# Fused attention and two gated layers on one core: partial outputs kept apart until the last layer, gated values split out of PSUM, and new costs in the planner

## The chip, the core and the metric

The kernel runs on one core of a Trainium2 chip. The metric is device time in microseconds (us) of one execution. The core has TensorE (PE, with PEld for its weight loads), VectorE (DVE), ScalarE (ACT), GpSimd (POOL), and SyncE (SP), whose queue here issues nearly every DMA. Engines run their own instructions strictly in program order and wait for each other through semaphores.

## The reference

Three parts follow each other on float32 data; the weights arrive as float64.

```
q_rot, k_rot = rotate(q), rotate(k)                       # 4 batches, 8 heads, 576 tokens, 64 wide
attn = softmax(q_rot @ k_rot.T / 8);  x = attn @ v        # x: 2304 tokens x 512
gate = 1 / (1 + exp(-(x @ w_gate)));  val = x @ w_val     # 512 -> 1536
y = (gate * val) @ w_out                                  # 1536 -> 512
h = y @ w_in;  e = exp(h - max(h));  solu = h * e / sum(e)     # 512 -> 1024
ln = (solu - mean) / sqrt(var + 1e-6) * g_ln
out = ln @ w_out2                                         # 1024 -> 512
```

## The kernel before, in words

Every matmul operand is held as a high part and a low part, and each product is three matmuls (high by high, high by low, low by high). So each value that PE is to read costs two instructions: a cast that writes the high part, and a subtraction that writes the low part.

**Stage A** (0 to some 303 us) is attention and is not touched. Its output goes to memory as `xd`, in three blocks of 768 tokens.

**Stage B** (some 303 to 800 us) is the gated layer. The 1536 inner columns are done in three passes `s` of 512, each pass over three blocks `b`: nine blocks. A block has four units: the gate product of half of the columns, the value product of that half, and again both for the other half (`unit`). After the first block a unit is seven block products of a Strassen scheme (`product`, 42 matmuls of 384 columns), whose intermediate sums ACT copies out of PSUM (`hold`, line 994, tiles `held`) and DVE adds back in PSUM (`finish`, line 999, and line 1049). PSUM has two sets of four banks a to d: `near` for gate units, `far` for value units. ACT takes the sigmoid into `sg`; DVE multiplies the value bank into `sg` (line 1013), and `sg` is split into `gs`: the high part by ACT or DVE (line 487), the low part by POOL or DVE (line 1018). Then two outputs of 48 matmuls each (`output`) project the two halves of the block's tokens, the first in the near banks, the second in the far ones. For `s` = 0 ACT copies each output bank into one of six slots of `yst` (line 1085), which SP stores to memory as `yd` (line 1086). For `s` > 0 SP first loads the sum so far from `yd` into the slot (line 1082), DVE adds the bank (line 1083), and SP stores it again.

Between blocks SP loads the next block's `x` into `xst` (line 962), DVE forms Strassen differences (line 536), and the pieces are split into `xs` (541, 543 high, 545 low). At each new `s` the weights are decoded from float64 (464 on ACT; 467, 470, 475 on DVE), added (484) and split (487 high, 495 and 958 low).

**Stage C** (some 790 us to the end) is the last layer on 18 tiles of 128 tokens: load of `y` (1120), split (1129 high, 1131 low), 24 matmuls into `ph` ("H"), six steps of exponential and normalisation ("n", lines 1268 to 1292), a DMA transposition of packed halves ("P", "u"), and 24 matmuls into `po` ("J").

**Order.** In stage B and the start of C every instruction is a `job` with an engine, a cost, the spans it reads and writes and a due time; `run_jobs` replays the jobs with these costs and writes the program in that order. `AV` is a job that may go to ACT or DVE, `GV` one for POOL or DVE; it goes to whichever is free first by these costs. Stage C is then written by a string, `START`, and a loop over tiles.

Of the kernel before, what the change touches and what calls it, by code (L numbers as in the profile page):

```python
# [20 lines left out]
def kernel(  # L21
# [21 lines left out]
    nc = tc.nc  # L43
# [300 lines left out]
    def scale_x(i):  # L344
# [8 lines left out]
    xd, yd = (  # L353
        [hbm.tile([KD * P * BT], F32, name=f"{n}{b}").rearrange("(k p t) -> k p t", k=KD, p=P) for b in range(NB)] for n in ("xd", "yd")
# [492 lines left out]

    jobs, seen = [], {}

    def job(eng, took, fn, reads=(), writes=(), need=0.0):  # L850
# [8 lines left out]
        jobs.append((eng, took, fn, after, need))  # L859
# [33 lines left out]
    HURRY = 3.0  # L893
    raws_used = [0]

    def decode(kind, n, dst, dst_at, need):
# [14 lines left out]
    def make_sums(need):  # L911
        for n, (out, x, y, _) in enumerate(SUMS):
            job(V, 0.45, lambda n=n: w_sum(n, V), (w32_at(x), w32_at(y)), (w32_at(out),), need - 4)

    def make_splits(k, parts, need, of=None):
        for to, c in parts:
            at_ = to if of is None else of + to
            src, hi, lo = one("w32", at_, at_ + c), words_at(W_SLOTS[k], c, to), words_at(W_SLOTS[k], c, 1792 + to)
            job(AV, (0.1 + c / 1000, 0.08 + c / 1500), lambda e, to=to, c=c, at_=at_: w_high(slots[k], to, c, at_, e), (src,), (hi,), need - 3)
            job(GV, (0.2 + c / 430, 0.08 + c / 930), lambda e, to=to, c=c, at_=at_: w_low(slots[k], to, c, e, at_), (src, hi), (lo,), need - 2)  # L920
# [27 lines left out]
    def make_unit(kind, n, where, need):  # L948
# [8 lines left out]
        job(AV, (0.58, 0.42), lambda e: high(e, t[:, 0], val), (at_,), (hi,), need - 3)  # L957
        job(GV, (1.35, 0.62), lambda e: e.tensor_sub(out=t[:, 1], in0=val, in1=t[:, 0].bitcast(F32)), (at_, hi), (lo,), need - 2)

    def load_x(b, need):  # L960
        for kk in range(KD):
            job(SP, 1.3, lambda kk=kk: nc.sync.dma_start(out=xst[kk], in_=xd[b][kk]), (one(f"xd{b}"),), (one("xst", 2 * kk, 2 * kk + 2),), need - 6)
# [3 lines left out]
    def quarter_at(name, j):  # L966
        k, t = {"B11": (0, 0), "B12": (0, 1), "B21": (1, 0), "B22": (1, 1)}[name]
        return one("xst", 2 * (2 * k + j) + t, 2 * (2 * k + j) + t + 1)

    def split_x(need):  # L970
        for n, (name, at_, of) in enumerate(X_STEPS):
            for j in range(2):
                here = quarter_at(at_, j)
                if of is not None:
                    use = {2: 2, 4: 3, 6: 3, 8: 4}[n]
                    job(V, 0.5, lambda n=n, j=j: x_step(xst, n, j, t_eng=V), tuple(quarter_at(q, j) for q in of), (here,), need + use - 4)
# [200 lines left out]
    for c in range(12, 16):  # L1177
        make_unit("p", c % 8, C_AT[c], END + 40)
# [312 lines left out]
```

## Time and profile before

| | |
|---|---|
| time, three runs | 990.88, 992.06 (median), 995.15 us |
| the profiled execution, its own time | 995.61 us |
| span from its first to its last instruction | 993.8 us |
| busy: PE, PEld, DVE, ACT, POOL | 917.2, 854.8, 782.5, 620.2, 511.4 us |
| mean granted TensorE clock | 0.975 |

The profiled execution is 3.55 us above the median of the runs; 1.8 us of it lie around the span. A share of busy time is a mean over three stages with different limits, so the stages are read one by one.

### The profile page before, as it was taken

How to read it: one execution, taken by the hardware profiler on the slowest of the kernel's cores; microseconds unless marked ns; L12 is line 12 of the kernel's file. 1: busy time of each engine (PE TensorE's matmuls, PEld its weight loads, DVE VectorE, ACT ScalarE, POOL GpSimd, SP SyncE). 2: the span in 40 equal slices, each digit the busy share in tenths (PEclk: the TensorE clock that was granted, in tenths of full speed). 3: DMA queues.
4: the chain of work that ended last, by engine and by line, in shares of the span. 5: the costliest groups of instructions: out<-in, count | busy, mean ns of one | idle time of the engine just before them, and what ended most of it. 6: DMA issues, size and time to landing. Idle time of an engine off the chain costs nothing.

```text
span 993.8 us, 16167 instructions
## 1 busy us (share of the span) xinstructions
PE 917.2 (92%) x5368; PEld 854.8 (86%) x5368; DVE 782.5 (79%) x1298; ACT 620.2 (62%) x1288; POOL 511.4 (51%) x411
## 2 busy tenths in 40 slices
PE   5999999999999689997998988898999889999998
PEld 4999999989989679996998988797999868888886
DVE  6999999999885968599784879894779776666661
ACT  5999999889873535554743445461537656656662
POOL 7688898889562645475550547471437411112110
PEclk9999999999999889999999999999999899999999
DMA  5668777877626551424533251816054444544532
GB/s 138 154 174 214 189 196 190 219 187 180 179 81 210 172 165 53 137 76 144 180 100 112 73 160 47 274 63 202 12 166 141 155 106 97 122 89 98 115 69 48
DMA packets 128403, 136.33 MB, mean 137 GB/s; under 512 B 54832, under 2 KB 106304, under 8 KB 128320
## 3 DMA queue, kind: packets, MB, share of 16 engines
q1 hardware_dynamic: 128320, 135.30, 48.9%
q8 instruction: 42, 0.69, 0.3%
q14 instruction: 41, 0.34, 0.1%
HBM read 75.67 MB, written 25.76 MB: 102 GB/s over the span
## 4 chain that ended last, share of the span: by engine, by line
PE 57%; DVE 21%; DMA 8%; issue 7%; ACT 6%; POOL 0%; SPq 0%; DVEq 0%; ACTq 0%; POOLq 0%
PE s L292 8%; PE av L420 7%; PE te L379 5%; DVE xst L536 4%; PE po L1353 3%; PE po L1351 3%; PE po L1352 3%; DMA yd<-yst 2%; PE ph L1258 2%; PE ph L1256 2%; PE ph L1257 2%; DVE xs L545 2%; DVE w L484 2%; PE tq L219 2%; DVE sg L1013 2%
## 5 line engine op out<-in xcount | busy, mean ns | idle before, releaser
L1018 POOL TENSOR_TENSOR gs<-sg,gs 128x384 fp32r<-128x384 f32 x60 | 71.3, 1193 | 87.7 <-ACT gs L487 77.2
L304 ACT ACTIVATE e<-s,nm 128x576 f32<-128x576 f32 x144 | 107.5, 747 | 13.6 <-DVE nm L299 13.3
L299 DVE TENSOR_REDUCE nm<-s 128x1 f32<-128x576 f32 x144 | 107.2, 745 | 4.5 <-PE s L292 2.9
L373 DVE TENSOR_TENSOR et<-te,et 128x512 fp32r<-128x512 f32 x144 | 98.5, 685 | 12.6 <-ACT et L370 12.3
L292 PE MATMUL s<-st 128*128 128x288 f32 x512 | 100.0, 318 | 6.8 <-ACT e L304 5.3
L420 PE MATMUL av<-et,vs 128*128 128x288 f32 x512 | 100.0, 316 | 0.6 <-DVE uw L660 0.3
L545 POOL TENSOR_TENSOR xs<-xst,xs 128x384 fp32r<-128x384 f32 x71 | 84.5, 1208 | 31.1 <-ACT xs L541 14.0
L370 ACT CAST et<-te 128x512 fp32r<-128x512 f32 x144 | 84.1, 585 | 4.4 <-PE te L379 3.2
L379 PE MATMUL te<-ident,e 128*128 128x128 f32 x576 | 86.7, 274 | 0.0
L292 PEld LDWEIGHTS s<-st 128*128 128x128 f32 x512 | 74.4, 193 | 14.0 <-ACT e L304 9.9
L420 PEld LDWEIGHTS av<-et,vs 128*128 128x128 f32 x512 | 72.9, 189 | 4.3 <-DVE uw L660 2.8
L379 PEld LDWEIGHTS te<-ident,e 128*128 128x128 f32 x576 | 71.3, 142 | 0.1
L541 ACT CAST xs<-xst 128x384 fp32r<-128x384 f32 x97 | 47.0, 513 | 36.7 <-DVE xst L536 36.7
L1289 POOL TENSOR_TENSOR st<-st,mhalf 128x1 f32<-128x1 f32 x18 | 10.4, 579 | 100.2 <-DVE st L1288 100.2
L464 ACT ACTIVATE mag<-raw_w 128x512 f32<-128x512 f32 x52 | 34.7, 675 | 41.8 <-DMA raw_w<-in_moe_w_val_dram 18.7
L536 DVE TENSOR_TENSOR xst<-xst 128x384 f32<-128x384 f32 x64 | 59.4, 959 | 0.0
L495 POOL TENSOR_TENSOR wg<-w,wg 128x512 fp32r<-128x512 f32 (+2 forms) x16 | 24.6, 1539 | 56.5 <-ACT wg L487 37.0
L721 PE MATMUL near_a<-xs,wg 128*128 128x384 f32 x96 | 35.0, 364 | 16.7 <-ACT held L994 14.2
L487 ACT CAST gs<-sg 128x384 fp32r<-128x384 f32 x65 | 33.2, 515 | 25.7 <-DVE sg L1013 25.4
L1131 POOL TENSOR_TENSOR xs<-xst,xs 128x512 fp32r<-128x512 f32 x18 | 24.6, 1367 | 44.0 <-ACT xs L1129 43.4
L432 POOL TENSOR_TENSOR x_sb<-uw,um 64x576 f32<-64x576 f32 x30 | 43.7, 1456 | 3.3 <-DMA um<-uw 2.0
L169 POOL TENSOR_TENSOR turned_t<-raw_t,other_t 128x576 f32<-128x576 f32 (+1 forms) x30 | 43.7, 1479 | 1.2
(340 smaller groups left out, 3111.8 us busy)
## 6 DMA issues: line engine op xcount, KB each, us to landing
yd<-yst SPq DMA_DIRECT2D x72, 192.0 KB
st<-st SPq DMA_DIRECT2D x45, 288.0 KB
xst<-xd SPq DMA_DIRECT2D x32, 384.0 KB
raw_w<-in_moe_w_out_dram SPq DMA_DIRECT2D x20, 512.0 KB
yst<-yd SPq DMA_DIRECT2D x48, 192.0 KB
st<-st SPq DMA_DIRECT2D x47, 144.0 KB
raw_w<-in_moe_w_gate_dram SPq DMA_DIRECT2D x12, 512.0 KB
raw_w<-in_moe_w_val_dram SPq DMA_DIRECT2D x12, 512.0 KB
```

The lines of the kernel that those rows point to most:

```text
L169: op(out=turned[i][:, sl, hs, here].rearrange("p i h d -> p h i d"), in0=raws[i][:, hs, sl, here], in1=others[i][:, hs, sl, there],)
L292: nc.tensor.matmul(ps[:, j, :HALF], w, x, start=m == 0, stop=m == len(mm) - 1)
L299: nc.vector.tensor_reduce(out=nm, in_=ps[:, :, :HALF], axis=AX.XY, op=ALU.max, negate=True)
L304: nc.scalar.activation(out=e.rearrange("p (j c) -> p j c", j=2), in_=ps[:, :, :HALF], func=AF.Exp, bias=nm, accum_out=sums[i][:, n:n + 1],)
L370: nc.scalar.copy(out=h_out, in_=ps)
L373: nc.vector.tensor_sub(out=l_out, in0=ps, in1=h_out.bitcast(F32))
L379: nc.tensor.transpose(ps[:, r * P:(r + 1) * P], e[:, r * P:(r + 1) * P], ident)
L420: nc.tensor.matmul(av[:, :HALF], *mm[m], start=m == 0, stop=m == len(mm) - 1)
L536: t_eng.tensor_sub(out=here, in0=x, in1=y)
L541: nc.scalar.copy(out=t[:, 0], in_=here)
L545: l_eng.tensor_sub(out=t[:, 1], in0=here, in1=t[:, 0].bitcast(F32))
L1018: job(GV, (1.05, 0.5), lambda e: e.tensor_sub(out=out[:, 1], in0=t, in1=out[:, 0].bitcast(F32)), (at_, hi), (lo,), y_need - 2)
```

## The change

- **Partial outputs stay apart.** `yd` becomes three arrays, one for each `s`. An output bank is now only copied into its slot, for all `s` (an `AV` job), and stored; no load and no add stand in stage B. In stage C each tile loads three arrays into three stages of `xst`, and two additions (line 1127, POOL or DVE in the plan, POOL in the loop) sum them before the split. The last block's output is copied into `sg`.
- **Gated values are split from PSUM.** DVE multiplies in place in the value bank (line 1015); ACT casts the high part from the bank (1018), and DVE subtracts the low part from the bank (1019). POOL, which cannot do this, has no part in it any more.
- **The planner** gets new costs, a flag for jobs that use a port shared by DVE and POOL (a second such job is planned to start only when the first has ended), POOL takes a job only when DVE has 3 us of work waiting, `hold` has its due time 8 earlier, and latencies between engines differ by engine.
- **Start of stage C.** The two outputs of the last block come before the first H; five tiles instead of two are in the plan, `START` is gone, and the loop runs with one tile more ahead (`AHEAD` 5, `LAG` 4).

```diff
-            job(V, 0.56, lambda: nc.vector.tensor_mul(out=t, in0=src, in1=t), (src_at, at_), (at_,), need)
+            job(V, 0.47, lambda: nc.vector.tensor_mul(out=src, in0=src, in1=t), (src_at, at_), (src_at,), need)
             out = gs[f, half]
-            job(AV, (0.48, 0.34), lambda e: high(e, out[:, 0], t), (at_,), (hi,), y_need - 3)
-            job(GV, (1.05, 0.5), lambda e: e.tensor_sub(out=out[:, 1], in0=t, in1=out[:, 0].bitcast(F32)), (at_, hi), (lo,), y_need - 2)
+            job(A, 0.41, lambda: nc.scalar.copy(out=out[:, 0], in_=src), (src_at,), (hi,), need + 1)
+            job(V, 0.47, lambda: nc.vector.tensor_sub(out=out[:, 1], in0=src, in1=out[:, 0].bitcast(F32)), (src_at, hi), (lo,), need + 2)
...
-            if s:
-                job(SP, 0.7, lambda t=t, mem=mem: nc.sync.dma_start(out=t, in_=mem), (mem_at,), (at_,), need + 2)
-                job(V, 0.56, lambda t=t, x=x: nc.vector.tensor_add(out=t, in0=bank[x], in1=t), (bk, at_), (at_,), need + 8 + 0.2 * m)
-            else:
-                job(A, 0.48, lambda t=t, x=x: nc.scalar.copy(out=t, in_=bank[x]), (bk,), (at_,), need + 8 + 0.2 * m)
-            job(SP, 0.7, lambda t=t, mem=mem: nc.sync.dma_start(out=mem, in_=t), (at_,), (mem_at,), need + 14)
+            job(AV, (0.41, 0.47), lambda e, t=t, x=x: high(e, t, bank[x]), (bk,), (at_,), need + 8 + 0.2 * m)
+            job(SP, 0.65, lambda t=t, mem=mem: nc.sync.dma_start(out=mem, in_=t), (at_,), (mem_at,), need + 14)
...
+        for s in range(3):
+            job(SP, 1.0, lambda s=s: load_y(t, s), (one(f"yd{s}_0", 0, 8),), (st_at[s],), need - 8)
+        for s in range(1, 3):
+            job(GV, (1.33, 0.6), lambda e, s=s: sum_y(t, s, e), (st_at[0], st_at[s]), (st_at[0],), need - 4)
...
+                elif e is G and found:
+                    t = max(free[id(e)], min(x[0] for x in found))
+                    if free[id(V)] - t + sum(took_on(x[1], V) for x in ready[id(V)] if x[0] <= t) < BACKLOG:
+                        continue
...
+                at_ = [(max(x[0], free[id(e)], port if (e is V or e is G) and jobs[x[1]][5] else 0.0), x) for x in found]
...
-    START = 'X H2 P0 n2 n2 n2 L5 H3 n2 T P1 u0 n2 n2 u0 n3 n3 H4 n3 u0 P2 Y5 L6 n3 u1 J0 n4 n3 n4 n3 P3 n4 u1 n4 u1 n4 n4 P4'
```

Over the whole program the plan moves these counts. Low parts of `xs`: POOL 71 to 32, DVE 41 to 80. Low parts of weights (lines 495 and 958): POOL 57 to 9, DVE 11 to 59. Low parts of `gs`: POOL 60 to 0, DVE 12 to 72. Copies of output banks: 24 on ACT become 42 on ACT and 30 on DVE, the last eight of the 72 into `sg`; 48 additions on DVE go. High parts on DVE (487 and 543): 26 to 16. Additions of `y` in the plan: 9 on DVE.

On SP's queue, between the first and the second block of pass `s` = 1 (the loads of the next `x`, the stores of the four near and four far banks, and the loads of the sum so far), the rows before are:

```order
L962 DMA xst<-xd_145 128x768 x2
L457 DMA raw_w_4696<-in_moe_w_val_dram 128x4x128
L962 DMA xst<-xd_145 128x768 x2
L1086 DMA yd_146<-yst 128x384 x4
L1082 DMA yst<-yd_146 128x384 x2
L1082 DMA yst<-yd_147 128x384
L1086 DMA yd_146<-yst 128x384
L1082 DMA yst<-yd_147 128x384
L1086 DMA yd_146<-yst 128x384 x3
```

Of the change, at the same place:

```order
L964 DMA xst<-xd_145 128x768 x2
L1086 DMA yd_0_149<-yst 128x384 x4
L964 DMA xst<-xd_145 128x768 x2
L458 DMA raw_w_65<-in_moe_w_val_dram 128x4x128
L458 DMA raw_w_4702<-in_moe_w_val_dram 128x4x128
L1086 DMA yd_0_149<-yst 128x384 x4
```

The loads of `yst` are gone, and the near stores stand ahead of two of the four loads of `x` instead of behind all four.

On DVE, at the same boundary and through the second unit of the new block, the rows before are:

```order
L1083 TENSOR_TENSOR yst<-far_c,yst 128x384
L999 TENSOR_TENSOR near_b<-near_b,held_4718 128x384
L1083 TENSOR_TENSOR yst<-far_d,yst 128x384
L999 TENSOR_TENSOR near_c<-near_c,held_u 128x384
L1049 TENSOR_TENSOR near_d<-near_a,held_4721 128x384
L999 TENSOR_TENSOR near_a<-near_a,held_4719 128x384
L999 TENSOR_TENSOR far_b<-far_b,held_4718 128x384
L1013 TENSOR_TENSOR sg<-far_b,sg 128x384
L487 CAST gs_0_4709<-sg 128x384
L1018 TENSOR_TENSOR gs_0_4709<-sg,gs_0_4709 128x384
```

Of the change:

```order
L488 COPY yst<-far_d 128x384
L1001 TENSOR_TENSOR near_b<-near_b,held_4724 128x384
L1001 TENSOR_TENSOR near_c<-near_c,held_u 128x384
L1050 TENSOR_TENSOR near_d<-near_a,held_4727 128x384
L1001 TENSOR_TENSOR near_a<-near_a,held_4725 128x384
L1001 TENSOR_TENSOR far_b<-far_b,held_4724 128x384
L1015 TENSOR_TENSOR far_b<-far_b,sg 128x384
L1019 TENSOR_TENSOR gs_0_4715<-far_b,gs_0_4715 128x384
L1001 TENSOR_TENSOR far_c<-far_c,held_u 128x384
L1015 TENSOR_TENSOR far_c<-far_c,sg 128x384
L1050 TENSOR_TENSOR far_d<-far_a,held_4727 128x384
L1015 TENSOR_TENSOR far_d<-far_d,sg 128x384
```

The additions that need a loaded slot no longer stand ahead of `near_b`, the copy of `far_c` is ACT's, and the low part of a gated value (line 1019) stands right behind the multiplication (line 1015), or one to three rows behind it; ACT's cast lies between the two in time.

## Rows read from the trace of the kernel before

**Rows 1.** Busy time by stretch: us, PE, PEld, DVE, ACT, POOL, clock, DMA share, GB/s
```profile
303.00:786.00 483.00, 432.83 (x2363) 421.64 (x2363) 386.09 (x593) 240.78 (x505) 241.14 (x189) 0.96 0.40 130
786.00:831.00 45.00, 40.47 (x171) 34.60 (x171) 29.99 (x56) 24.98 (x36) 8.82 (x9) 0.91 0.53 145
831.00:976.00 145.00, 145.00 (x642) 120.09 (x641) 91.38 (x175) 92.26 (x121) 22.69 (x26) 1.00 0.44 94
417.00:474.00 57.00, 47.87 (x266) 46.03 (x267) 53.87 (x76) 31.71 (x68) 36.34 (x27) 0.97 0.37 119
```
**Rows 2.** Waits of PE from 303 us on: us in total, times, longest
```profile
PE near_a L721 <- ACT held L994: 14.2, 6, 5.6
PE near_c L721 <- ACT held L994: 13.8, 7, 4.7
PE near_a L1068 <- ACT gs L487: 4.3, 2, 3.5
PE near_a L1068 <- DVE gs L487: 3.7, 2, 1.9
PE far_a L1068 <- DVE yst L1083: 3.7, 1, 3.7
PE near_a L1069 <- DVE wo L958: 3.4, 1, 3.4
PE po L1353 <- DVE xs L1320: 2.8, 1, 2.8
```
**Rows 3.** PE in order of time: start, us, what, idle before and releaser
```profile
473.50 0.69 PE L721 MATMUL near_a<-xs,wg 128*128 128x384 f32 x1 [5.58 <-ACT held L994]
...
528.46 0.69 PE L721 MATMUL near_c<-xs,wg 128*128 128x384 f32 x1 [4.49 <-ACT held L994]
528.95 0.52 PE L722 MATMUL near_c<-xs,wg 128*128 128x384 f32 x1
```
**Rows 4.** DVE's and SP's queue before that wait, in order of time
```profile
526.42 0.56 DVE L1083 TENSOR_TENSOR yst<-far_c,yst 128x384 f32<-128x384 f32 x1 [7.31 <-DMA yst<-yd]
...
516.03 3.33 SPq L1086 DMA_DIRECT2D yd<-yst  x4
523.69 2.07 SPq L1082 DMA_DIRECT2D yst<-yd  x3
```
**Rows 5.** Waits of all engines from 303 us on
```profile
POOL gs L1018 <- ACT gs L487: 77.2, 28, 27.5
...
DVE yst L1083 <- DMA yst<-yd: 27.1, 7, 9.6
...
DVE w L484 <- DMA w<-wd: 7.3, 1, 7.3
```
**Rows 6.** DVE by line, 303 to 800 us: count, busy us, mean ns, idle before
```profile
L536 DVE TENSOR_TENSOR xst<-xst 128x384 f32<-128x384 f32 x64 | 59.4, 959 | 0.0
L545 DVE TENSOR_TENSOR xs<-xst,xs 128x384 fp32r<-128x384 f32 x41 | 39.1, 982 | 0.0
L484 DVE TENSOR_TENSOR w<-w 128x256 f32<-128x256 f32 x48 | 32.8, 683 | 8.2 <-DMA w<-wd 7.3
...
L475 DVE SCALAR_TENSOR_TENSOR rawv<-raw_w,rawv 128x512 int32<-128x512 int32 x27 | 22.2, 828 | 0.3
L470 DVE SCALAR_TENSOR_TENSOR w<-mag,w 128x512 int32<-128x512 int32 x19 | 20.0, 1068 | 0.7 <-ACT mag L464 0.3
```
**Rows 7.** Single lines: duration in ns, min/median/max, first and last start
```profile
L536 DVE TENSOR_TENSOR xst<-xst x64: 541/901/2158, 337.3 to 722.7; 128x384 f32<-128x384 f32 x64
L484 DVE TENSOR_TENSOR w<-w x48: 406/426/1522, 331.0 to 631.7; 128x256 f32<-128x256 f32 x48
L475 DVE SCALAR_TENSOR_TENSOR rawv<-raw_w,rawv x28: 674/690/1548, 327.1 to 802.1; 128x512 int32<-128x512 int32 x28
L1013 DVE TENSOR_TENSOR sg<-far_c,sg x18: 543/546/558, 322.9 to 763.2; 128x384 f32<-128x384 f32 x18
L1131 POOL TENSOR_TENSOR xs<-xst,xs x18: 1285/1296/1745, 758.4 to 949.0; 128x512 fp32r<-128x512 f32 x18
```

More of the change, by code (lines that the diff above doesn't have):

```diff
@@ L1174, with bank_h, job_n @@
-    job_y(2, END + 27)
-    job_y(3, END + 32)
-    job_y(4, END + 38)
+    FIRST_C = 5
+    def bank_h(t):
+        return one("bank", 2 * (t % 2), 2 * (t % 2) + 2)
+    def job_n(t, need):
+        ph_at = bank_h(t)
+        e_at = one("yst", 1024 * t, 1024 * t + 1024) if t < 2 else one(f"h{(t - 2) % 3}")
+        junk_at = [one(f"sg{n // 4}{'abcd'[n % 4]}") for n in range(3 * t, 3 * t + 3)] if t < 2 else [one("j")]
+        x = [one("X")] if t > 1 else []
+        m, r = one(f"max{t}"), one(f"rv{t}")
+        step = lambda: do("n", t)
+        job(V, 1.13, step, (ph_at,), (m,), need, False)
+        job(A, 1.15, step, [ph_at, m] + x, (e_at,), need + 1.5)
+        job(V, 1.15, step, (ph_at, e_at), (e_at,), need + 3, False)
+        job(A, 1.15, step, (e_at,), junk_at + [r], need + 5)
+        job(V, 0.3, step, (r,), (r,), need + 7, False)
+        job(V, 0.85, step, (r, e_at), (e_at,), need + 9, True)
@@ new lines, in job_j @@
+    def job_j(t, need):
+        lt = LT_AT[t % 2]
+        for half in range(2):
+            units = [words_at(C_AT[8 + f], 1024) for f in range(4 * half, 4 * half + 4)]
+            at_ = one(f"po{t % 2}")
+            job(nc.tensor, 2.73, lambda half=half: project(t, half), [words_at(lt, 2048), one("X")] + units + ([at_] if half else []), (at_,), need + 2.7 * half)
+        job(A, 0.6, lambda: project_out(t), (at_,), (), need + 8)
+    H_AT = [END + 5.5 * t for t in range(FIRST_C)]
+    for half in range(2):
+        output(*LAST, half, half)
@@ new lines @@
+    for t in range(FIRST_C):
+        job_y(t, H_AT[t])
+        job_h(t, H_AT[t])
+        if t == 2:
+            names = [f"gs{f}{half}" for f in range(FG) for half in range(2)]
+            names += [f"sg{p_}{x}" for p_ in range(2) for x in "abcd"] + ["held1", "held5", "heldu", "held4"]
+            job(V, 0.01, lambda: open_pools(), (), [one(n, 0, 2) for n in names] + [one("xs4", 0, 4 * HT), one("bank", 4, 8), one("X")], END + 9, False)
+            for n in range(2):
+                job_p(n, H_AT[n] + 5.5)
+        job_n(t, H_AT[t] + 5.5)
+        if t == FIRST_C - 1:
+            job_u(0, END + 6 + 5 * t)
+        if t > 1:
+            job_p(t, H_AT[t] + 5.5)
@@ L1177 @@
+    for n in range(2):
+        job_y(FIRST_C + n, END + 33 + 5 * n)
     for c in range(12, 16):
-        make_unit("p", c % 8, C_AT[c], END + 40)
+        make_unit("p", c % 8, C_AT[c], END + 30)
     def run_jobs():
@@ L1398, in do @@
         elif kind == "Y":
+            for n in range(1, 3):
+                sum_y(t, n, nc.gpsimd)
             split_y(t)
         elif kind == "P":
-            pack(t)
+            if t not in packs:
+                packs[t] = pack(t)
+            next(packs[t])
         elif kind == "J":
@@ L1406, in do @@
             project(t, 1)
+            project_out(t)
         elif kind == "L":
-            load_y(t)
+            for n in range(3):
+                load_y(t, n)
         elif kind == "X":
@@ L1438 @@
         if t < NTT - 1:
-            pack(t)
+            for _ in range(3):
+                do("P", t)
         do("J", t - AHEAD)
```

182 lines of the change are left out of this document (95 added, 87 removed).

## The prediction

> **What bounds the kernel now.** I read the busy time by stretch first, then PE's waits, then the queue behind the largest of them, then what the busiest other engine spends its time on.
>
> The stretches say where time can be had. In the loop of stage C PE is busy 145.00 of 145 us at full clock [rows 1]: nothing is to be had there, and nothing is lost unless another engine becomes slower than PE. In stage B (303 to 786 us, 483 us) PE is busy 432.8 us, so it idles 50 us, and its mean clock is 0.96. So what the change can bring lies in B and at the start of C (786 to 831 us: PE 40.5 of 45, clock 0.91).
>
> PE's waits say what ends the idle time. 28.0 us in 13 waits end with ACT's copy `held` (14.2 and 13.8), 8.0 us with a high part of `gs`, 3.4 with the last output weight, 3.7 with an addition into `yst`, 2.8 in C [rows 2]. But `held` is a copy of 0.5 us; the question is what it was late for. At 528.46 the PE row shows 4.49 us of idle time [rows 3]. Just before, DVE had stood 7.31 us at `yst<-far_c` for the reload of a partial sum; SP issued four stores at 516.03 and could issue that reload only at 523.69, since a reload into a slot must wait until the store out of it has landed [rows 4]. `near_b` stands behind that addition on DVE, ACT's next sigmoid behind `near_b`, and the `held` copies behind the sigmoid: one late DMA holds three in-order queues. Such waits on DVE come to 27.1 us in 7 places [rows 5].
>
> The other large wait, 5.58 us at 473.50 [rows 3], is of another sort. It closes the block in which weights are made, and there DVE is busy 53.87 of 57 us [rows 1]. DVE is the bound there, and much of its time is not its own work: the Strassen difference of 384 columns takes between 541 and 2158 ns, 959 on average [rows 6, 7]. The multiplication of the same 384 columns with one operand in PSUM keeps to 543 to 558 ns [rows 7]. POOL is busy 241 of the 483 us [rows 1]. So operations on SBUF alone get longer beside POOL, those with a PSUM operand don't.
>
> The Trainium skill ("SBUF — State Buffer", section "SBUF: two separate sides") states this as a lock: VectorE with two SBUF inputs and GpSimd share a pair of ports, and whoever comes second waits out the other's whole instruction. The rows agree on which operations suffer.
>
> **The change, part by part.** The sum is made against the profiled execution (995.6 us) and then carried over to the median of the runs, 992.06.
>
> *Reloads and additions.* 48 loads, 48 additions and DVE's 27.1 us of waiting go from B. What is late next is the slot: eight banks go through six slots, so the seventh copy waits for the store of the first. But that store is issued an output earlier, and now ahead of two loads of `x`. Without the reload of 2 to 3 us behind it I leave 0.5 us for each of the four boundaries. It stays on ACT's queue ahead of `held`, so a late store would still reach PE.
>
> *Low parts from POOL to DVE.* DVE gains 60 low parts of `gs`, priced at 0.55 us by the nearest row with a PSUM operand (line 1013, [rows 7]): 33.0 us. It gains 39 low parts of `xs` at 0.54 (minimum of line 536, [rows 7]): 21.1. Of 48 low parts of weights some 40 lie in B, at 0.68 (median of line 475, 512 columns, [rows 7]): 27.2. It gains 26 copies of banks in B at 0.55: 14.3; it loses 42 additions in B at 0.55: 23.1. Together +72.5 us.
>
> *Contention.* What POOL costs DVE now: line 536, 64 times (0.959 less 0.541), 26.8 us; line 545, 41 times (0.982 less 0.541), 18.1; line 484, 48 times (0.683 less 0.406), 13.3 [rows 6, 7]. The 139 decode instructions lie between line 475's excess (0.828 less 0.674) and line 470's (1.068 less 0.674): 21 to 55 us; I take 35. Together 93 us. POOL's two-input instructions in the plan fall from 188 to 41, 22%. If what is left costs in proportion, 20 us stay and 73 go. By the skill's lock each of the 41 could hold DVE for its whole length (241.14 us for 189, [rows 1], 1.28 us): 52 us instead of 20, which would take the sum to some 32 us more.
>
> So DVE's sum in B stays as it is: 386 + 72.5 - 73. This is the step I had least expected: the change frees POOL, not DVE. What it takes from B are DVE's waits: 27.1 for reloads, and of the 7.3 for the kept weights `wd` [rows 5] half, since one of these loads now stands ahead of the stores. By DVE's account B gets 27.1 + 3.6 + 0.5 = 31 us shorter.
>
> *PE's account.* Of the 28.0 us behind `held` the weight blocks keep theirs (two, 5.58 shown), and the rest, 28.0 - 11 = 17, falls to some 4: -13. Of 8.0 us behind `gs` half goes, since a low part takes 0.55 on DVE instead of 1.28 on POOL: -4. The 3.7 at the last output goes, since the two H that filled DVE's queue ahead of it now come later. `wo`, 3.4: -1. That is 22 us. The clock: 0.04 of 483 us is 19 us of clock missing, a part of it in idle time; behind the 4.49 us wait the matmuls show 0.52 us instead of 0.33 or 0.34, half the pace, 1.2 instead of 2.4 GHz [rows 3]. I put the lost work at 14 us, and 10 of it at waits that vanish or halve. -32 us. The two accounts agree; I take **-33**.
>
> *Stage C's loop.* POOL gets two additions of 1.30 us a tile (line 1131, [rows 7]); 13 tiles fit the 145 us (26 POOL instructions, two a tile), so +34 us on 22.7 [rows 1]. Even if each of these blocked DVE for as long, DVE would come to 91.4 + 34 = 125 of 145 us, and PE covers it. If that cover failed, each us above PE's pace would count 13 times. Two more loads of 256 KB in 11.2 us are 47 GB/s on 94, so a DMA share of at most 0.66 on 0.44 [rows 1].
>
> *Start of C.* DVE is busy 30.0 of 45 us there [rows 1] and gets nine additions of `y` and eight low parts of weights at 0.68, 11.6 us: nearly full. Five H in a row give PE cover of some 26 us before the first J, which needs all of DVE's weight work. I bound this at -4 to +8 us and take 0.
>
> *ACT*: 240.8 of 483 us busy [rows 1]; casts and copies that move there are covered by its idle time, except where DVE waits for them (below).
>
> **Forecast: faster, 992.06 - 33 = 959 us**, chance 0.60, between 946 and 972: the ends are 13 us each way, from the decode bounds (21 and 55 for 35) and the start of C.
>
> **Rivals.**
>
> *The wait for the cast moves from POOL to DVE.* POOL stood 77.2 us in 28 waits for ACT's cast of `gs` [rows 5]. That was free, since POOL had nothing urgent behind it. Now the low part waits on DVE, and behind it `near_b`, the next differences, everything. For it: the new order has only none to three DVE instructions between multiplication and low part, about the time of a cast. Against it: ACT is half idle. If each of the 72 comes 0.3 us late, 22 us are given back: **981 us** (972 to 987), chance 0.20.
>
> *Slower: the value bank is held too long.* The bank is now free only after multiplication, cast and low part, at least 0.5 + 0.55 us later than before, and the next product in the same bank set comes after one gate unit, 42 matmuls, some 7.6 us (47.87 us for 266, [rows 1]). If DVE's queue makes the low part of the last bank (`far_a`) come later than that, PE stands at the next value unit or output, 18 times a run. It decides for slower from 38/18 = 2.1 us each; at 2.5 us it gives 45 us: 959 + 45 = **1004 us**, chance 0.08. The skill's advice to evacuate PSUM promptly ("PSUM — Partial Sum Buffer", section "Summary: rules for kernel authors") speaks for this rival; no row of before shows such a wait.
>
> *The change doesn't do what it says: the plan's port rule misses.* The planner's clock has no stalls in it, so DVE and POOL meet anyway. If 60% of the 93 us stay instead of 22%, 35 us come back: **994 us**, no difference, chance 0.06.
>
> *Better: the weight blocks lose their waits too* (11 us, with clock 6 more): **942 us**, chance 0.06.
>
> **How the numbers follow.** Faster is the forecast, the first and the last rival: 0.86. A measurement of this kernel can tell about 0.5%, 5 us. Same 0.06, slower 0.08. The range from 940 to 986 holds the forecast's 0.60, most of the cast rival and of the better case, some 0.82.
>
> **What would show it.** Right: no wait of DVE on a DMA into `yst`, and no PE wait over 1 us at the three boundaries inside passes 1 and 2; line 537 (the differences) near 0.6 us on average; DVE's busy time in B still near 386 us but B 30 us shorter; fewer stretches at the low clock. Wrong: DVE idle ahead of line 1019 for ACT's cast, some 20 us or more in sum (first rival); PE waiting in `far_a` for line 1019 (second); line 537 still near 0.9 us (third); PE no longer full in C's loop, or over 15 us of waits before the first J.

## The result and the profile after

The changed kernel takes 957.91 us (median of four runs, 957.73 to 958.54), the kernel before 991.89 beside it: ratio 0.965, 95% interval 0.963 to 0.968. The forecast was 959. The profiled execution took 958.54 us, its span 956.8 against 993.8, 37.0 us less.

The total was right, but not as the sum had it: that it came within 2 us is luck, for two errors of some 30 us with opposite signs cancelled. PE's timeline gives the boundaries: the first matmul of the first output (332.70 before, 329.03 after), the end of stage B's last output (796.54 before, where two H of 10.92 us already stand inside, and 719.89 after), the H from which the loop is counted here (868.52 before, the tenth tile's, 797.50 after, the ninth's), the start of the last J's (961.00 and 913.16). The view by stretch, with the columns of [rows 1], of the kernel before:

```profile
332.70:762.58 429.88, 385.99 (x2114) 377.68 (x2114) 343.12 (x523) 210.78 (x453) 215.63 (x171) 0.96 0.38 123
762.58:796.54 33.96, 30.28 (x145) 28.04 (x145) 27.07 (x51) 21.75 (x36) 20.46 (x16) 0.90 0.51 169
796.54:868.52 71.98, 67.45 (x290) 55.12 (x289) 49.29 (x91) 45.00 (x62) 11.40 (x12) 0.98 0.46 104
868.52:961.00 92.48, 92.48 (x410) 76.60 (x408) 58.20 (x116) 58.44 (x80) 15.30 (x17) 1.00 0.44 94
```

and of the changed one:

```profile
329.03:719.89 390.86, 385.18 (x2209) 382.46 (x2209) 343.39 (x662) 229.27 (x491) 45.08 (x38) 1.00 0.40 127
719.89:797.50 77.61, 66.17 (x265) 51.68 (x265) 64.75 (x116) 48.29 (x71) 20.28 (x19) 0.93 0.51 129
797.50:913.16 115.66, 107.69 (x457) 84.35 (x456) 80.39 (x124) 63.88 (x86) 41.46 (x37) 1.00 0.55 128
913.16:956.70 43.54, 36.45 (x153) 28.50 (x151) 14.87 (x24) 17.57 (x22) 1.10 (x2) 0.96 0.24 55
303.00:719.89 416.89, 410.58 (x2354) 407.54 (x2353) 363.45 (x696) 242.25 (x516) 47.45 (x39) 1.00 0.42 135
```

**Stage B** shrank from 452.9 us (332.70 to 796.54 less the two H) to 390.9, and began 3.7 us earlier: 65.7 us gained, not 33. PE is now busy 385 of 391 us at full clock. Of the 65.7, PE's idle time gives 41.9 (47.6 us before without the two H, 5.7 now), the same matmuls at a higher granted clock 20.2 (busy 405.4 before, 385.2 now), the earlier start 3.7. **Stage C**, all H and J, grew from 208.2 us to 236.9: 28.7 us lost, not 0. Its loop, 145.00 of 145 before, is busy 107.7 of 115.7. 65.7 less 28.7 is the 37.0.

PE's waits from 303 to 720 us (us in all, times, longest), which answer to [rows 2]: the 28.0 us behind `held` have become 1.9 with `held_u`, at the weight blocks too.

```profile
PE near_a L1069 <- ACT wo L488: 2.4, 1, 2.4
PE near_a L1070 <- DVE wo L960: 1.2, 2, 0.8
PE near_a L722 <- ACT held L996: 1.1, 2, 0.5
PE near_a L722 <- ACT held_u L996: 0.8, 1, 0.8
```

DVE by line from 303 to 720 us (columns of [rows 6]):

```profile
L546 DVE TENSOR_TENSOR xs<-xst,xs 128x384 fp32r<-128x384 f32 x80 | 45.9, 617 | 0.0
L537 DVE TENSOR_TENSOR xst<-xst 128x384 f32<-128x384 f32 x64 | 38.7, 631 | 0.3
L485 DVE TENSOR_TENSOR w<-w 128x256 f32<-128x256 f32 x48 | 20.3, 424 | 1.5
...
L1019 DVE TENSOR_TENSOR gs<-far_b,gs 128x384 fp32r<-128x384 f32 x18 | 9.9, 552 | 1.5 <-ACT gs L1018 1.5
```

The differences fell from 959 ns to 631, the weight sums from 683 to 424 [rows 6].

PE's waits from 719 us on come to 21.8 us (before, those for `ph` and `po` came to 4.5), and more than half are for the split of `y`, the cast (1136) and the low part (1138):

```profile
PE ph L1316 <- ACT xs L1136: 6.5, 7, 3.7
PE ph L1318 <- POOL xs L1138: 5.2, 9, 0.6
PE ph L1316 <- DVE st L1352: 3.5, 1, 3.5
PE po L1416 <- DVE xs L1383: 3.2, 4, 1.6
```

But the split is not what is slow. DVE by line in the loop, 797.5 to 913.16 us:

```profile
L1353 DVE TENSOR_SCALAR e<-e,st 128x1024 f32<-128x1024 f32 x9 | 14.7, 1633 | 0.3
...
L1336 DVE SCALAR_TENSOR_TENSOR e<-ph,e 128x1024 f32<-128x1024 f32 x10 | 12.2, 1218 | 0.0
...
L1386 DVE COPY z<-tp 128x1024 uint16<-128x1024 uint16 x9 | 9.0, 998 | 0.0
L1352 DVE TENSOR_TENSOR st<-st 128x1 f32<-128x1 f32 x9 | 6.8, 759 | 6.0 <-POOL st L1350 6.0
L1386 DVE COPY pk<-e 128x1024 uint16<-128x1024 uint16 x4 | 4.7, 1180 | 0.1
```

and before, 868.5 to 961 us, the same operations:

```profile
L1275 DVE SCALAR_TENSOR_TENSOR e<-ph,e 128x1024 f32<-128x1024 f32 x9 | 11.0, 1219 | 0.1
...
L1292 DVE TENSOR_SCALAR e<-e,st 128x1024 f32<-128x1024 f32 x9 | 7.3, 813 | 0.3
L1323 DVE COPY z<-tp 128x1024 uint16<-128x1024 uint16 x9 | 6.8, 754 | 0.0
L1323 DVE COPY pk<-e 128x1024 uint16<-128x1024 uint16 x9 | 6.2, 694 | 0.3
...
L1291 DVE TENSOR_TENSOR st<-st 128x1 f32<-128x1 f32 x9 | 1.4, 160 | 6.0 <-POOL st L1289 6.0
```

The normalisation doubled, and a product of one column takes 759 ns instead of 160; the operation that reads PSUM (1336) is as before. The timeline of one tile after, DVE's and POOL's rows, shows who stands beside them:

```profile
864.94 1.82 DVE L1353 TENSOR_SCALAR e<-e,st 128x1024 f32<-128x1024 f32 x1
866.80 1.67 DVE L1386 COPY pk<-e 128x1024 uint16<-128x1024 uint16 x1
...
864.16 0.55 POOL L1350 TENSOR_TENSOR st<-st,mhalf 128x1 f32<-128x1 f32 x1 [5.42 <-DVE st L1349]
864.93 2.98 POOL L1127 TENSOR_TENSOR xst<-xst 128x512 f32<-128x512 f32 x2 [0.22 <-DMA xst<-yd]
```

In POOL's queue the two additions stand directly behind the power (1350), which DVE's normalisation waits for too. In seven of eleven tiles the additions start as the power ends; in the other four, as here, they wait another 0.2 to 1.5 us for a load. DVE loses 1.0 us at 1353 and 1.0 at the copy here (2.0 us a tile on average by the lines above), and the copy on ACT, the output copy and the cast of `y` behind it come later. Before, DVE's cycle was already close to PE's. Two tiles in which DVE doesn't wait for PE:

```profile
867.59 1.23 DVE L1320 TENSOR_TENSOR xs<-z,xs 128x1024 fp32r<-128x1024 f32 x1 [1.97 <-ACT xs L1319]
878.06 1.23 DVE L1320 TENSOR_TENSOR xs<-z,xs 128x1024 fp32r<-128x1024 f32 x1 [1.98 <-ACT xs L1319]
```

10.47 us a tile, of which DVE is busy 6.8 (58.20 of 92.48 us): the rest is waiting, in turn, for ACT and POOL. PE needs 10.88. So the slack was 0.4 us, and 10.47 + 2.0 is 12.5; the tiles after come 12.13 us apart on average (nine from 797.50 to 906.71).

### The profile page after: what moved, and what is told of

The parts are those of the page before. It is cut to its first block, busy times and chain, and to the rows that moved or that the text cites. A ratio compares the mean times of both kernels' runs of the same rounds, so it can differ in the third digit from the quotient of the medians.

```text
span 956.8 us, 16031 instructions
## 1 busy us (share of the span) xinstructions
PE 907.0 (95%) x5368; PEld 840.3 (88%) x5368; DVE 796.4 (83%) x1432; ACT 631.6 (66%) x1315; POOL 349.2 (36%) x285
## 4 chain that ended last, share of the span: by engine, by line
PE 54%; DVE 19%; issue 11%; ACT 6%; DMA 6%; POOL 2%; SPq 1%; POOLq 0%; DVEq 0%; ACTq 0%
PE s L292 8%; PE av L421 7%; PE te L380 5%; DMA xst<-yd 3%; DVE e L1353 2%; PE tq L219 2%; PE near_a L722 1%; PE near_a L723 1%; PE near_a L724 1%; DVE st L1352 1%; PE tk L401 1%; PE far_a L722 1%; PE far_a L724 1%; PE far_a L723 1%; ACT z L1386 1%
## 5 line engine op out<-in xcount | busy, mean ns | idle before, releaser
L546 POOL TENSOR_TENSOR xs<-xst,xs 128x384 fp32r<-128x384 f32 x32 | 36.1, 1153 | 201.9 <-ACT xs L542 126.7
L542 ACT CAST xs<-xst 128x384 fp32r<-128x384 f32 x102 | 49.6, 516 | 19.6 <-DVE xst L537 18.1
L1127 POOL TENSOR_TENSOR xst<-xst 128x512 f32<-128x512 f32 x27 | 36.8, 1365 | 50.0 <-DMA xst<-yd 49.2
L1316 PE MATMUL ph<-wg,xs 128*128 128x512 f32 x90 | 36.9, 410 | 11.9 <-ACT xs L1136 6.5
L1383 DVE TENSOR_TENSOR xs<-z,xs 128x1024 fp32r<-128x1024 f32 x17 | 20.8, 1225 | 30.7 <-ACT xs L1382 30.7
L546 DVE TENSOR_TENSOR xs<-xst,xs 128x384 fp32r<-128x384 f32 x80 | 45.9, 617 | 0.0
L465 ACT ACTIVATE mag<-raw_w 128x512 f32<-128x512 f32 x52 | 35.0, 674 | 12.5 <-DMA raw_w<-in_moe_w_out_dram 6.0
L1318 PE MATMUL ph<-wg,xs 128*128 128x512 f32 x90 | 37.0, 411 | 5.3 <-POOL xs L1138 5.2
L537 DVE TENSOR_TENSOR xst<-xst 128x384 f32<-128x384 f32 x64 | 38.7, 631 | 0.3
```

The costliest lines, as they stand in the source:

```text
L537: t_eng.tensor_sub(out=here, in0=x, in1=y)
L542: nc.scalar.copy(out=t[:, 0], in_=here)
L546: l_eng.tensor_sub(out=t[:, 1], in0=here, in1=t[:, 0].bitcast(F32))
```

## The experiments

Each is compared with the kernel before in the same session; B (first output to first H; before, the end of the last output less the two H) and C (the rest, to the end of the span) are worked out from PE's timeline as above, in us. The three attempts at the start of C are not in the table, since H stands between outputs there.

| kernel | time | ratio, 95% interval | B | C |
|---|---|---|---|---|
| before | 991.9 | 1 | 452.9 | 208.2 |
| changed | 957.9 | 0.965 (0.963 to 0.968) | 390.9 | 236.9 |
| no additions in C's loop | 939.6 | 0.950 (0.946 to 0.953) | 389.9 | 216.9 |
| split a tile earlier | 968.5 | 0.979 (0.976 to 0.981) | 389.7 | 245.9 |
| ring | 942.4 | 0.952 (0.950 to 0.955) | 391.6 | 220.0 |
| ring, reordered | 944.7 | 0.955 (0.951 to 0.958) | 390.7 | 220.3 |
| additions on DVE | 944.1 | 0.955 (0.951 to 0.958) | 388.9 | 222.0 |
| reloads back | 941.1 | 0.951 (0.949 to 0.953) | 396.0 | 213.1 |
| no rules on POOL | 990.9 | 1.001 (0.999 to 1.002) | 421.2 | 238.6 |
| no rules, gated values from SBUF | 1003.0 | 1.013 (1.010 to 1.016) | 430.6 | 239.6 |
| 64 idle POOL subtractions | 970.3 | 0.978 (0.976 to 0.980) | 403.7 | 234.9 |

### Why stage C's loop got slower

**No additions** (the kernel leaves them out).

```diff
-            for n in range(1, 3):
-                sum_y(t, n, nc.gpsimd)
             split_y(t)
```

> The changed kernel without the two additions per tile in stage C's loop (the three loads stay; so from tile 7 on the partial outputs of the second and third pass are left out of the result). In the changed kernel a tile of the loop takes 12.13 us on average (first matmuls of the tiles from 797.50 to 906.71 us, nine periods) instead of 10.88 before. Theory P (POOL's additions hold DVE: in each tile the 1024-column normalisation of line 1353 shows 1633 ns instead of 813, the packing copies 889 to 1180 instead of 694, the 128x1 product of line 1352 759 instead of 160): all of these go back, the loop runs at 10.88, the last J's lose their 5 us of excess too: 957.9 - 11 - 3 to 6, 940 to 944 us. Theory M (memory: three loads a tile land too late, or slow the transpositions): the loads are still there, the period stays above 11.8 and the time above 953.

Measured 939.6: every tile of the loop 10.88 us apart, lines 1353, 1386 and 1352 back at 813, 694 and 160 ns. The loads alone cost the loop nothing, so memory is out.

**The split a tile earlier.**

```diff
+    do("L", FIRST_C + 2)
     for t in range(FIRST_C, NTT + AHEAD):
+        if t + 3 < NTT:
+            do("L", t + 3)
         if t + 2 < NTT:
-            do("L", t + 2)
-        if FIRST_C + 1 < t + 1 < NTT:
-            do("Y", t + 1)
+            do("Y", t + 2)
```

> Loads, additions and split of a tile are written one whole iteration earlier (tile t+2 in iteration t instead of t+1; the third slot for split y was there), so that H can't wait for them. PE's waits in the changed loop are for the cast (line 1136) and the low part (line 1138) of y. Theory S (the split is late: load, two additions, cast and subtraction follow each other and H stands behind them): the waits vanish and the loop runs at 10.88: 940 to 944 us. Theory P (the additions hold DVE, and DVE's own cycle from row maximum to row maximum has become 10.47 + 2.0 = 12.45 us): the waits for lines 1136 and 1138 vanish but the period stays near 12.1, PE waits for DVE's release of ph or for the low part of the next J instead: 955 to 960 us.

968.5 us: the waits for 1136 and 1138 are gone, and most tiles come 12.59 us apart, slower than before the edit. Theory S falls. Now the operands are there in eight of eleven tiles, seven of them running; there the additions start at once behind the power, and the first catches the product of one column (998 ns on average, 759 in the changed kernel). Where loads are in time in the changed kernel, its row maxima too come 12.6 us apart (795.38, 807.99, 820.56); its mean of 12.13 owes to shorter distances around the late loads (11.56, 11.91, 10.58). DVE's and POOL's timeline of that kernel:

```profile
838.27 1.24 DVE L1352 TENSOR_TENSOR st<-st 128x1 f32<-128x1 f32 x1 [0.66 <-POOL st L1350]
839.54 1.86 DVE L1353 TENSOR_SCALAR e<-e,st 128x1024 f32<-128x1024 f32 x1
...
837.68 0.55 POOL L1350 TENSOR_TENSOR st<-st,mhalf 128x1 f32<-128x1 f32 x1 [5.42 <-DVE st L1349]
838.20 2.65 POOL L1127 TENSOR_TENSOR xst<-xst 128x512 f32<-128x512 f32 x2
```

The first addition runs from 838.20 to about 839.5, the product ends at 839.51; the second holds line 1353. PE waits for the low and high part of J's operand instead, as P said, at a higher price than it gave; one wait of 9.6 us, where the loop begins, came on top.

**The ring: additions at another time.** A third stage, and additions of tile t+2 directly behind the split of t+1:

```diff
+            own = (yst_t[:, 1024:1536], yst_t[:, 1536:2048], xst_t[:, 0:512])[t % 3]
...
         elif kind == "Y":
+            split_y(t)
+        elif kind == "S":
             for n in range(1, 3):
                 sum_y(t, n, nc.gpsimd)
-            split_y(t)
...
-        if t + 2 < NTT:
-            do("L", t + 2)
+        if t + 3 < NTT:
+            do("L", t + 3)
         if FIRST_C + 1 < t + 1 < NTT:
             do("Y", t + 1)
+        if t + 2 < NTT:
+            do("S", t + 2)
```

> A third stage for the loads (ring in free parts of xst and yst), so that loads come one tile earlier and POOL's two additions of tile t+2 stand ahead of the power of tile t, right behind the subtraction of tile t+1, some 6 us before DVE's normalisation and packing copy. Same instructions, other time. Theory P: lines 1353, 1352 and 1386 go back to 813, 160 and about 700 ns, but the additions now lie beside DVE's subtraction of line 1383 (two operands in SBUF, 1226 ns), which gets up to 1.3 us longer: DVE's cycle 10.5 to 11.8 instead of 12.45, 944 to 953 us. Theory S: the split has 5 us more and the loop runs at 10.88: 940 to 944, with line 1383 as before.

942.4 us with the same instructions: 10.88 a tile. DVE by line in the loop of that kernel:

```profile
L1387 DVE TENSOR_TENSOR xs<-z,xs 128x1024 fp32r<-128x1024 f32 x11 | 14.3, 1304 | 11.4 <-ACT xs L1386 11.2
...
L1357 DVE TENSOR_SCALAR e<-e,st 128x1024 f32<-128x1024 f32 x10 | 8.1, 813 | 0.4
```

The subtraction (1387 there) got only 0.08 us longer, not 1.3; the addition beside it was the one that gave way. The time lies in S's range, not in P's, but S had fallen with the run before: P's price for the new place was too high, its cause stands.

**The ring with another order of steps** (the exponential ahead of ACT's cast, DVE's subtraction behind the multiplication):

```diff
-        for x in 'uunununnnn':
+        for x in 'uunnununnn':
```

> As the ring, and the order of steps in an iteration is changed so that the exponential stands ahead of the cast of line 1382 on ACT, and DVE's subtraction of line 1383 behind the multiplication of line 1336, where DVE idles for ACT's square. The additions then lie beside DVE's operations with a PSUM operand (1329, 1336). Theory P: nothing of DVE's is held; cycle below 10.88, so PE is the bound of the loop again: 957.9 - 11.3 (loop) - 3 to 8 (the tiles ahead of it and the last J's), 938 to 944 us. If DVE is held all the same, or the later subtraction makes J late: 946 or more.

944.7 us; the intervals of the two rings overlap and their spans agree (942.0 and 941.9). The loop was at PE's pace already. The time lies between the two ranges, and P's "nothing of DVE's is held" missed: the subtraction was held after all (1508 ns against 1226), where it cost nothing.

**Additions on DVE.**

```diff
-                sum_y(t, n, nc.gpsimd)
+                sum_y(t, n, nc.vector)
```

> In stage C's loop DVE makes the two additions itself instead of POOL (some 690 ns each, as line 1127 takes on DVE in the plan). Theory P (POOL's additions hold DVE for 2.0 us a tile): DVE does 1.4 us more and is held 2.0 us less, its cycle goes from 12.45 to 11.85 us: a little faster, 950 to 956 us. If DVE is simply the engine with too much to do: 1.4 us a tile more, 970 us or more.

944.1 us: DVE gets more to do and the kernel gets faster, by 1.1% by the ratios. Better than P's 950 to 956, since part of the 1.4 us fits into DVE's wait for the cast of line 1382 (1.30 us a tile, 1.97 before): row maximum to row maximum is 11.14 us (836.27 to 847.41), not 11.85. That is still over PE's 10.88, which PE keeps for six tiles before it falls to some 11.1 in the last ones.

### What gave stage B its 62 us

**Reloads back**: the change without its first part.

```diff
...
-            job(AV, (0.41, 0.47), lambda e, t=t, x=x: high(e, t, bank[x]), (bk,), (at_,), need + 8 + 0.2 * m)
+            if s:
+                job(SP, 0.65, lambda t=t, mem=mem: nc.sync.dma_start(out=t, in_=mem), (mem_at,), (at_,), need + 2)
+                job(V, 0.47, lambda t=t, x=x: nc.vector.tensor_add(out=t, in0=bank[x], in1=t), (bk, at_), (at_,), need + 8 + 0.2 * m)
+            else:
+                job(AV, (0.41, 0.47), lambda e, t=t, x=x: high(e, t, bank[x]), (bk,), (at_,), need + 8 + 0.2 * m)
...
```

> Of the changed kernel, the first part alone is undone: stage B loads the sum so far, adds and stores it again as before, and stage C loads one array and adds nothing; gated values, planner rules and costs stay. Stage C should then run as without its additions (939.6 us in that run, -18). For stage B: theory R (the prediction's: the reloads cost what DVE waited for them, 27.1 us, and 42 additions where 26 copies were): B some 31 us longer than the 390.9 of the changed kernel, 957.9 - 18 + 31 = 971 us. Theory K (the reloads were late only because POOL's and DVE's shared work had made everything late; with DVE's contention gone they land in time or DVE has slack to wait): B at most 8 us longer, 948 us or less.

941.1 us. Without its largest part the change is some 15 us faster (1.5% by the ratios, 16.9 us by the medians): C gets 23.8 back, B loses 5.1. With the reloads and the same wait for a store to land, DVE now waits for them this long:

```profile
DVE yst L1088 <- DMA yst<-yd: 6.4, 4, 3.0
```

against 27.1 in 7 [rows 5]. Theory R, my own, falls. What made the reload of [rows 4] late stands in DVE's rows ahead of the four stores at 516.03, in the kernel before:

```profile
507.60 3.48 DVE L536 TENSOR_TENSOR xst<-xst 128x384 f32<-128x384 f32 x3
511.01 2.65 DVE L545 TENSOR_TENSOR xs<-xst,xs 128x384 fp32r<-128x384 f32 x2
...
515.45 0.55 DVE L1083 TENSOR_TENSOR yst<-near_a,yst 128x384 f32<-128x384 f32 x1
```

PE's last matmul into `near_a` starts at 508.13, and DVE adds that bank 7.3 us later. Among what stands ahead of it are five operations on SBUF that take 6.1 us, where five of 0.541 us take 2.7; POOL is at work beside them. So 3.4 us of the lateness that the wait of 7.31 us inherits are contention. The order of SP's queue has changed as well, and its share was not separated.

**No rules on POOL.**

```diff
-    HURRY, BACKLOG = 3.0, 3.0
+    HURRY, BACKLOG = 3.0, -1e9
...
-                at_ = [(max(x[0], free[id(e)], port if (e is V or e is G) and jobs[x[1]][5] else 0.0), x) for x in found]
+                at_ = [(max(x[0], free[id(e)]), x) for x in found]
```

> Of the changed kernel, the planner's two rules on POOL are undone (no second two-input job is held back while one runs, POOL takes what it is free for); POOL's low parts in the plan rise from some 40 to 75, gated values and partial outputs stay as changed. Theory R (contention per POOL instruction is what was read from before, 93 us for 188 POOL instructions, 0.5 us each, and DVE gives away 35 instructions of 0.6): DVE's sum even, time 955 to 962 us. Theory K (contention is what makes PE wait, since it hits DVE where it is late): B 8 to 25 us longer, 966 to 983 us.

990.9 us, no difference from the kernel before: undoing the two rules costs 30.3 us of B, more than either theory gave (K: 8 to 25), and the wait for `held` is back (9.9 us in 5 at `near_a`). DVE and POOL by line, from 303 us to the end of B at 749.60:

```profile
L537 DVE TENSOR_TENSOR xst<-xst 128x384 f32<-128x384 f32 x64 | 62.3, 1015 | 0.0
...
L485 DVE TENSOR_TENSOR w<-w 128x256 f32<-128x256 f32 x48 | 27.1, 564 | 4.2 <-DMA w<-wd 3.1
...
L546 POOL TENSOR_TENSOR xs<-xst,xs 128x384 fp32r<-128x384 f32 x75 | 85.4, 1161 | 128.5 <-ACT xs L542 48.4 <-DVE xs L544 34.2 <-issue 27.7
```

**No rules, and gated values split from SBUF** by POOL or DVE as before:

```diff
-            job(V, 0.47, lambda: nc.vector.tensor_mul(out=src, in0=src, in1=t), (src_at, at_), (src_at,), need)
+            job(V, 0.47, lambda: nc.vector.tensor_mul(out=t, in0=src, in1=t), (src_at, at_), (at_,), need)
...
+            job(AV, (0.41, 0.27), lambda e: high(e, out[:, 0], t), (at_,), (hi,), y_need - 3)
+            job(GV, (1.01, 0.47), lambda e: e.tensor_sub(out=out[:, 1], in0=t, in1=out[:, 0].bitcast(F32)), (at_, hi), (lo,), y_need - 2)
```

> As the kernel without the rules on POOL, and the gated values are split from SBUF again by whichever of POOL and DVE is free (POOL some 120 low parts in the plan, of 188 before); only the partial outputs stay apart. So this is the first part of the change nearly alone. Theory R (the first part gives 27 to 31 of stage B's gain, the rest only moves work): B 5 to 35 us longer than 390.9, most of it where DVE is nearly full at the weight blocks; 975 to 990 us. Theory K (the reload waits were a consequence): most of B's gain of 62 us is lost, 1000 us or more.

1003.0 us, as K had it. Another 9.4 us of B go with the gated values, 39.7 of the 62 in all (R: 5 to 35). What stays, partial outputs kept apart with POOL busy, is 1.3% slower than before as a whole: B 22.3 us better, C 31.4 worse.

**Idle POOL work**: the plan unchanged, POOL disturbed.

```diff
-            job(A, 0.41, lambda: nc.scalar.copy(out=held[x], in_=bank[of]), (pb(of),), (one("held" + x),), need - 8)
+            def copy_and_load():
+                nc.scalar.copy(out=held[x], in_=bank[of])
+                if x in "14":
+                    nc.gpsimd.tensor_sub(out=scratch, in0=held[x], in1=held[x])
+
+            job(A, 0.41, copy_and_load, (pb(of),), (one("held" + x),), need - 8)
```

> The changed kernel, its plan untouched, and 64 additional subtractions of 384 columns on POOL in stage B (after ACT's copies held 1 and held 4 of each unit, into a tile that nobody reads): POOL's two-input instructions in B go from 39 to some 103, the number of the kernel without the rules on POOL, but no DVE instruction is taken off and no order changes. Theory K (POOL's instructions themselves hold DVE): at 0.5 us each, the price read from before, DVE gets 32 us more work; it idles some 50 us of B, so between a third and all of it reaches PE: B 10 to 32 us longer, 968 to 990 us, and the differences of line 537 and the decode lines longer than in the changed kernel, the operations with a PSUM operand (lines 1001, 1015, 1019) not. Rival O (the rules helped by another order of the plan, not by fewer collisions): B as in the changed kernel within 5 us, 958 to 963.

970.3 us, B 12.8 longer. By line, 303 to 735 us:

```profile
L537 DVE TENSOR_TENSOR xst<-xst 128x384 f32<-128x384 f32 x64 | 36.4, 594 | 0.3
L485 DVE TENSOR_TENSOR w<-w 128x256 f32<-128x256 f32 x48 | 24.5, 510 | 1.5
...
L496 DVE TENSOR_TENSOR wv<-w,wv 128x512 fp32r<-128x512 f32 (+2 forms) x16 | 15.4, 975 | 0.0
...
L1025 DVE TENSOR_TENSOR gs<-far_c,gs 128x384 fp32r<-128x384 f32 x18 | 9.8, 547 | 0.0
...
L1000 POOL TENSOR_TENSOR scratch<-held 128x384 f32<-128x384 f32 x64 | 61.9, 967 | 277.7 <-ACT held L998 266.9 <-DVE gs L1025 4.4 <-DVE xs L546 3.8
```

POOL alone does slow B with no order changed; no wait of ACT names POOL, so it isn't that ACT's next copies wait until POOL has read a `held`. But 64 instructions here cost 12.8 us, while 73 more in the kernel without the rules (112 against 39 up to the end of B; the expectation's 103 counts only up to 722 us) cost 30.3 although they took 73 off DVE. The price doesn't go by their number. The time of DVE's instructions above the shortest of the same line and shape, added up from 303 us to the end of B, is 19 us in the changed kernel, 30 here and 70 without the rules (106 before). Without the rules the differences of line 537 alone hold 30 of it; here that line even got shorter, against my expectation, and the operations that read PSUM stay as ever (1025: 547 ns). Why these 64 hold DVE so little is not shown: half of their 62 us lies beside SBUF operations too.

### Three attempts at the start of stage C

All put H between the last two outputs on PE, so that one covers the latency of the other. The first does so on the kernel with the reloads.

```diff
...
-    for half in range(2):
-        output(*LAST, half, half)
...
+    output(*LAST, 0, 1)
     for t in range(FIRST_C):
...
+        if t == 1:
+            output(*LAST, 1, 1)
```

> As the kernel with the reloads back (941.1 us), and the start of stage C interleaved on PE: first output of the last block, the first two H, second output (again in the far banks), third H and on. In the kernel with the reloads PE loses 7.4 us in the first six H and 4.3 in the first J. If these are latencies of the first tiles' chains (H2 needs the bank of H0 back), the second output covers them: 934 to 938 us. Rival: the second output waits for the first one's copies out of the same banks and the chains are DVE's work, not latency: 940 to 944.

945.9 us (0.954, 0.952 to 0.955), outside both ranges and not faster than without it (0.951, 0.949 to 0.953; the intervals overlap). The output stands in the far banks directly behind the last value unit, and the wait that the second rival feared for the change appears here, made by this edit:

```profile
PE far_a L1069 <- DVE gs L1019: 5.2, 1, 5.2
```

The ring with the same order, and the loads and additions of tile 7 as jobs of the plan:

```diff
+    t = FIRST_C + 2
...
+        job(SP, 1.0, lambda s=s: load_y(t, s), (one(f"yd{s}_0", 0, 8),), (st_at[s],), END + 36)
...
+        job(GV, (1.33, 0.6), lambda e, s=s: sum_y(t, s, e), (st_at[0], st_at[s]), (st_at[0],), END + 46)
```

> As the ring kernel (942.4 us: partial outputs apart, POOL's additions moved), with the loads and additions of the first tile of the loop planned ahead of the loop's transpositions, and with the same interleaved start of stage C. The first should take 3 to 4 us (the wait of 3.9 for the cast of tile 7 behind DVE's 3.03 us wait for a power that stood behind additions that waited for a late load), the second up to 7: 932 to 938 us. Rival: no cover, as above: 938 to 942.

944.7 us (0.952, 0.950 to 0.954), as the ring; the same 5.2 us wait.

With two H ahead of the outputs and one between them, and C's first weights due earlier (on the kernel with the reloads):

```diff
...
-    for half in range(2):
-        output(*LAST, half, half)
...
     for t in range(FIRST_C):
         job_y(t, H_AT[t])
         job_h(t, H_AT[t])
+        if t in (1, 2):
+            output(*LAST, t - 1, 1)
```

> As the kernel with the reloads back (941.1 us), and another order on PE at the start of stage C: the first two H, first output of the last block, third H, second output, fourth H and on (both outputs in the far banks; in the interleaved kernel the output directly behind the last value unit waited 5.2 us for the low parts out of the far banks). If the start of C loses to latencies (first outputs to gated values, H2 to the bank of H0, second output to the copies out of the banks), the H in between cover them: of the 11.7 us that PE loses in the first seven H and two J with the reloads, 3 to 6 stay: 933 to 938 us. Rival: DVE is the bound there (gated values, the weights of C and the first normalisations meet in it), the waits only move: 940 to 946.

942.6 us (0.950, 0.948 to 0.952), the same as 941.1 with 0.951. The small waits went into one, PE for DVE's multiplication of an earlier H:

```profile
PE ph L1321 <- DVE e L1341: 7.6, 1, 7.6
```

The waits only moved, as the rival had it. That DVE is the bound there is likely (busy 78.4 of 91 us from 695 to 786 us) but not shown.

The best kernels of this study that leave nothing out are the change without its first part (941.1; 942.6 with H first) and the change with a ring (942.4), which do not differ measurably: 5% below before, 1.3 to 1.6% below the change by the ratios (the median of before was 989.3 to 992.5 us from one session to the next).

## Why the prediction was right in the total, and wrong in two terms

**Contention, 93 us down to 20: right in size.** By the same reckoning, what POOL still costs DVE is 5.8 us at line 537 (0.631 less 0.541, 64 times), 6.1 at 546 (80 times 0.076), 0.9 at 485, and 4.5 at the decode lines: 17. Line 467, which the 139 decode instructions include, has one tensor as input and was held too: its mean fell from 0.65 to 0.42 us.

**"What it takes from B are DVE's waits": the step that failed in stage B.** I let the contention cancel against the work that moves to DVE and credited the gain to the reloads, 27.1 us. With the reloads back and the rules kept, B is 5.1 us longer; with the reloads gone and the rules undone, 30.3. The late reload was in large part a symptom: the store ahead of it waited for a DVE that was late, by 3.4 us of contention in the rows shown, and I followed the chain to the store's landing and no further. An equal sum of DVE's busy time was no argument either, nor did the sum stay: of 386 us (303 to 786) 363.5 are left (303 to 719.89), in part since contention fell by 86 us rather than 73 and DVE lost high parts that I had not counted. The contention had stretched the instructions in the middle of the chains; the work that came to DVE, low parts of 0.55 us, could use time in which it had idled: 97 us of B before (483 less 386, [rows 1]), 53 after (416.9 less 363.5).

**PE's account, -33: mis-sized, measured -65.7.** The weight blocks were to keep 11 us and `held` 4; 1.9 are left, the mechanism of the better rival. So idle time, 22 in the account, gave 41.9. The clock, 10, was put at half of its 0.04 of 483 us; it is at 1.00 throughout B and gave 20.2. (The half pace in [rows 3] shows in the distance of two starts, 0.32 us behind the wait and 0.17 ahead of it, not in 0.52 against 0.33.) The waits behind `gs`, put at half, are gone; `wo` kept 2.4 of 3.4 at line 1069, as foreseen, and 1.2 came at 1070. The sum itself has two slips: the 0.5 us left for each of four boundaries was never taken off, and -33 was taken where the accounts gave 31 and 32.

**Stage C's loop, 0: wrong, and the sentence behind it holds the mistake.** "Even if each of these blocked DVE for as long, DVE would come to 125 of 145 us, and PE covers it" compares a busy sum with a span. What had to be compared is DVE's cycle through ACT and POOL, 10.47 us, with PE's 10.88. The sign that it named, PE no longer full in C's loop, came. The price of the failed cover was told right: it counts each tile, 12.3 us over PE's pace from 797.50 to 913.16. The start of C, bounded by -4 to +8, lost 11.1 us more than before (17.8 over PE's pace up to 797.50, 6.7 before), and the last J's 5.3: with the loop, 28.7.

The Trainium skill ("SBUF — State Buffer", section "SBUF: two separate sides") has the lock in a wider form than I used: besides operations with two inputs in SBUF it names those in a two-port performance mode. The rows agree that operations with one tensor as input are held: the normalisation went from 813 to 1633 ns, the copies into `pk` from 694 to 1180. Whether they run in such a mode no row shows.

**The rivals.** The cast wait did not come: DVE idles 1.5 us ahead of 1019, not 20. The value bank is not held too long; no PE wait of the changed kernel names it. The rule that misses was false of this kernel, but its price, 994, is nearly what the kernel takes with the rules undone, 990.9. The better rival's mechanism was true, and stage C hid it.

**What stays open.** Which of the two rules carries how much was not tried. Undoing them changes the order of the plan too, so the 30.3 us of B are not the price of contention alone; the idle POOL work shows that contention alone has one. What the start of C loses was not explained, nor brought under the 6.7 us of before in any kernel. Between before and the kernel without rules and with gated values from SBUF, planner costs and due times differ too, so its 22.3 us of B are not the first part's alone: costs, due times and latencies were tried on their own nowhere. Shares also depend on the order in which parts are taken away: with the rules in place the reloads are worth 5.1 us, with POOL busy they may be worth more.

## What to carry to other kernels

Before adding work to an engine that looks half idle, measure its cycle through the other engines in one turn of the loop and compare that with the bound; a busy share says nothing about slack. When a wait ends with a late DMA, ask what made the DMA late: a stretched instruction three queues away looks like a memory problem. And time POOL's two-input work by what VectorE does beside it: the same additions cost 20 us of stage C or 3 (236.9 and 220.0 us against 216.9 without them), by their place in the queue, with loads a tile earlier.

## What was not expected of the hardware

One column is enough to be caught: a 128x1 product took 1240 ns instead of 160 behind an addition of 1.3 us on POOL. The lock works both ways: in the ring kernel POOL's addition that met DVE's subtraction took 2.16 us instead of 1.30, and DVE's only 1.32 instead of 1.23.
